# A recurrence fused with a two-layer MoE block: the first token sets worked in halves of four heads, and a plan with other transfer times

## The chip, the cores and the metric

The kernel runs on one core of one Trainium2 chip. The metric is the time on the device of one execution, in microseconds (us). A profiled execution is taken by the hardware profiler; its span runs from the first to the last instruction, and the execution's own time is a little longer.

The engines are named as in the profile: PE (matrix products; PEld its weight loads), DVE and ACT (elementwise work), POOL (elementwise work, here casts), SP (it issues the DMA transfers). Each takes its instructions in the order in which the program lists them, and an instruction that waits holds up those behind it.

## The reference

Inputs are q, k, v, alpha of shape 4 x 8 x 768 x 48 (batch, head, step, width) in float32, w_in (384 x 2048) and w_out (2048 x 384). Cut to what matters:

```python
def _attn_ref(q, k, v, alpha):
    state = np.zeros((B, H, D, D))
    for t in range(S):
        state = alpha[:, :, t, :, None] * state + np.einsum('bhd,bhe->bhde', k[:, :, t], v[:, :, t])
        y[:, :, t] = np.einsum('bhd,bhde->bhe', q[:, :, t], state)
    return y

def _moe_ref(x, w_in, w_out):
    r = np.maximum(x @ w_in, 0.0)
    return (r * r) @ w_out

x = attn_out.transpose(0, 2, 1, 3).reshape(B * S, H * D)     # 3072 tokens x 384
return _moe_ref(x, w_in, w_out)
```

## The kernel before

**Chunks.** The 3072 tokens are 24 chunks of 128, six to a batch. Within a chunk the recurrence is worked as products: L = ln(alpha), running sums of L over the tokens (a triangular matrix as stationary operand), A = exp(sum) and Ainv = exp(-sum), qA = q*A, kI = k*Ainv (scaling), scores = kI qA^T under a triangular mask (sm), and the outputs are sm times v plus qA times the state of the chunk before. The state is a product of kI and v, added in PSUM, scaled by exp of the chunk's total sum (ae) on DVE (L483, L660) and copied to bf16 on ACT (sb, L488, L665). The outputs are cast (xn), turned by PE and copied into xT_big (xT), the moving operand of the first MoE layer.

**Token sets.** The first four chunks come as two sets of 256 tokens (add_set, L336 on, loads in add_load2, L324 on). A set is loaded with two neighbouring tokens in one partition, so that a contiguous piece in memory is 384 bytes and not 192; j (0 or 1) names the even or the odd token. One load brings 384 KB: all eight heads, both j. add_set works by j: sums, exps and scalings for j = 0 and j = 1, transposes of q (L249) and of k for both j into one bank, copies (cast2, L409, L411) by j, scores by j, with all four head pairs of one j in a tile of two PSUM banks, and masked by mask_eo[j] (L452). The later chunks (add_chunk) are worked one by one.

**MoE.** The first layer (add_moe1) takes a group of chunks (GN: 4, 1, 1, 2, ...), and for each of 16 column blocks f of w_in makes three products of 128 x 256 (or 128) into a bank, relu on ACT (r, L744) and a square on DVE (gT, L753). Group 0 is worked as two pairs of chunks (lo = 0 and 2), and the products of pair 1 stand behind those of pair 0 in one chain. The second layer (add_moe2) makes for each chunk 16 products of 128 x 384 from gT and w_out; in group 0 it goes by quarters of four, each for all four chunks, so that the first quarter needs only the first quarter of w_out. The four chunks hold banks 4, 3, 2, 1 from their first quarter to their last.

**Weights.** w_in comes in five parts (column blocks 0 to 1, 2 to 3, 4 to 7, 8 to 11, 12 to 15), w_out in four; each is a load into one of four staging buffers and a cast to bf16 on POOL (load_w, L293, L296). The cast of a part gives its staging buffer back to the fourth load behind it.

**What sets the order.** A planner (class Plan) is run while the program is built. Every piece of work is an Op with an engine (or a choice of two), an assumed duration, dependencies, a priority and, where it needs one, a PSUM bank (takes; gives names the work that frees it). The planner takes the op that can start first, priority breaking ties, and the result, sorted by start, is the order of the program on all engines. The loads go through one planned DMA server in the order of DMA_ORDER, with assumed times LD (0.98, later LD1 = 1.0) for a load of one chunk, LD2 = 1.4 for a load of a set, WLD = 2.1 for a part of weights; SP issues them in that order. The times are assumed only in the plan: on the chip an instruction waits for what it really needs. A gate lets the recurrence run some 3.5 chunks ahead of the MoE work (LEAD).

**Opening.** PE first makes nine products on zeros into bank 4 (four columns of 128), and in planned gaps ahead of the first second-layer product more of 256 columns; their tile is named warm.

**PSUM.** Of eight banks, ps_sc holds the scores (two banks), ps_st the state (one), and banks[0] to banks[4] the rest: 0 and 1 for the recurrence (GLA_BANKS), 2 to 4 for the MoE.

The lines of the profile that the text speaks of: L331 (loads of a set), L318 (of a chunk), L293 and L296 (weights), L346 and L561 (Ln), L374 (exps of a set), L378 (its scalings), L351 (its cast of v), L246 and L249 (the helpers mm and tr, all products and all transposes).

Of the kernel before, what the change touches and what calls it, by code (L numbers as in the profile page):

```python
# [36 lines left out]
PE_CALM = 25.0  # L37


class Op:  # L40


    def __init__(self, eng, dur, emit, deps=(), prio=0.0, takes=None, gives=None, lat=None, at=0.0):
# [9 lines left out]
        self.start = self.done = None  # L53


def after(op, x=0.0):
    return (op, x)


class Plan:  # L60


    def __init__(self):
        self.pending = {}
        self.order = []
        self.free = {}

# [6 lines left out]
    def ready(self, op):  # L74
# [11 lines left out]
        if op.takes is not None:  # L86
            best = None
            for sl in op.takes:
                f = sl.free_at()
                if f is not None and (best is None or f < best):  # L90
                    best, op.slot = f, sl
            if best is None:
                return None
            t = max(t, best)
        return t

    def run(self, gate):
        free = self.free
        while any(self.pending.values()):
# [25 lines left out]
            op.start = t + getattr(op, "late", 0.0)  # L125
            free[eng] = t + op.dur
# [5 lines left out]
            if op.takes is not None:  # L132
                self.ready(op)
                op.slot.release.append(op.gives if op.gives is not None else op)
# [6 lines left out]
def kernel(  # L141
# [40 lines left out]
    ps_sc = ctx.enter_context(tc.tile_pool(name="ps_sc", bufs=1, space=PSUM))  # L182
    ps_st = ctx.enter_context(tc.tile_pool(name="ps_st", bufs=1, space=PSUM))
    banks = [ctx.enter_context(tc.tile_pool(name=f"bank{i}", bufs=1, space=PSUM)) for i in range(5)]
# [37 lines left out]
    mask_eo = [consts.tile([P, 1, 2, HP], BF16, name=f"mask{j}") for j in range(2)]  # L222
    for a in range(2):
        nc.vector.tensor_copy(mask_eo[0][:, 0, a, :], tri)
        nc.vector.tensor_copy(mask_eo[1][:, 0, a, :], tri if a else stri)
# [26 lines left out]
    sl_sc = Slots(1)  # L252
# [3 lines left out]
    GLA_BANKS = sl_bank[0:2]  # L256
    M1_BANKS = sl_bank[2:5]
    M2_BANKS = sl_bank[4:1:-1]

    def psum(op, shape, dt):  # L260
        i = op.slot.bank
        return banks[i].tile(shape, dt, name=f"bank{i}")
    X_SLACK = 0.2
    LD = 0.98
    LD1 = 1.0
    LD2 = 1.4
    WLD = 2.1
# [10 lines left out]
    def load_w(which):  # L278
# [19 lines left out]
        ld = add("DMA", WLD * n / 4 + 0.03, e_issue, prev, lat=2.0)  # L298
        op = add("POOL", 0.1 + 0.5 * n, e_cast, ld, prio=-3.0)
# [11 lines left out]
    def add_load(s, nm):  # L311
# [8 lines left out]
        d["ld_" + nm] = add("DMA", LD if s < 4 else LD1, ld, prev, lat=2.4 if s < 6 else 4.0, at=0.6)  # L320
# [3 lines left out]
    def add_load2(u, nm):  # L324
        d = E[u]

        def ld():
# [3 lines left out]
            pin(nc.sync.dma_start(out=t.rearrange("p (h e) -> p h e", h=H), in_=srcs2[nm][b, c // 2]))  # L331
        d["ld_" + nm] = add("DMA", LD2, ld, lat=2.5, at=0.6)

    def add_set(u):
# [7 lines left out]
        g = dict(prio=-10.0 + s0 * 0.01)  # L342
        R = [slice(HP * c, HP * c + HP) for c in range(2)]

        def e_ln():
            pin(nc.scalar.activation(L[:, :, :, 0:D], d["at"].rearrange("p h j d -> p j h d"), AF.Ln))  # L346
        ln = add("ACT", 0.85, e_ln, d["ld_at"], prio=-15.0)
# [4 lines left out]
        vb = add("POOL", 1.1, e_vb, d["ld_vt"], prio=-5.0)  # L352

        pm, A, Ai, exA, exI, mq, mk = {}, {}, {}, {}, {}, {}, {}

        def add_sum(j):
            def e_p0():
                pm[j] = psum(p0, [P, 512], FP32)
                cross = strict if j == 0 else incl
                mm(pm[j][:, 0:HD], lhsT=incl, rhs=L[:, 0, :, 0:D], start=True, stop=False)  # L360
                mm(pm[j][:, 0:HD], lhsT=(strict if j == 0 else incl), rhs=L[:, 1, :, 0:D], start=False, stop=True)
                if j == 0:
                    for p in range(NP):
                        for i in range(2):
                            mm(pm[j][:, HD + 2 * p:HD + 2 * p + 2], lhsT=L[:, i, 2 * p:2 * p + 2, :], rhs=half,
# [527 lines left out]
```

## Time and profile before

| | |
|---|---|
| runs | 193.73, 192.82, 193.62 us; median 193.62 |
| profiled execution | 192.82 us, span 191.1 us, mean granted clock of PE 0.997 |
| busy, share of the span | PE 95%, PEld 71%, DVE 68%, ACT 64%, POOL 14% |
| DMA | 30.22 MB, 158 GB/s in the mean; busy tenths 9 in the second to the twenty-fifth of 40 slices, but for two in between (7 and 8) |
| chain that ended last | PE 70%, DMA 15%, SP's queue 7%, DVE 2%, ACT 2% |
| ACT waits for alpha, chunks from the fifth on | 8.6 us in six waits, the longest 3.1 |

The page cuts the span into 40 slices of 4.78 us, with a digit for the busy tenths of each. PE's row is 7 to 9 in all but the last slice; in the first four slices a part of that is the products on zeros. The chain is followed back from the last instruction, at each step to what released it. In an answer by stretches each line has the stretch, its length and each engine's busy time, with the number of instructions in brackets. In a timeline a line has the start, the duration, the engine, the line of the kernel, the operation, out<-in and the shape; in square brackets stand the idle time before it and what ended it.

### The profile page before, as it was taken

How to read it: one execution, taken by the hardware profiler on the slowest of the kernel's cores; microseconds unless marked ns; L12 is line 12 of the kernel's file. 1: busy time of each engine (PE TensorE's matmuls, PEld its weight loads, DVE VectorE, ACT ScalarE, POOL GpSimd, SP SyncE). 2: the span in 40 equal slices, each digit the busy share in tenths (PEclk: the TensorE clock that was granted, in tenths of full speed). 3: DMA queues.
4: the chain of work that ended last, by engine and by line, in shares of the span. 5: the costliest groups of instructions: out<-in, count | busy, mean ns of one | idle time of the engine just before them, and what ended most of it. 6: DMA issues, size and time to landing. Idle time of an engine off the chain costs nothing.

```text
span 191.1 us, 5139 instructions
## 1 busy us (share of the span) xinstructions
PE 181.2 (95%) x2048; PEld 134.9 (71%) x2048; DVE 129.2 (68%) x280; ACT 121.6 (64%) x282; POOL 27.2 (14%) x44
## 2 busy tenths in 40 slices
PE   7887999989999799999999999999999999999992
PEld 2556788756887678767868768768778778668651
DVE  5478879634898888677878858758858858724200
ACT  3675589435986696854886956857857747628321
POOL 4015661641101111120110011011010000000000
PEclk9999999999999999999999999999999999999998
DMA  6999999999789999999999999860020020021012
GB/s 151 261 263 363 384 197 300 309 183 189 165 186 191 178 227 183 186 194 202 212 206 183 226 166 220 167 159 5 0 82 3 2 86 2 5 81 41 29 57 82
DMA packets 99176, 30.22 MB, mean 158 GB/s; under 512 B 92112, under 2 KB 98000, under 8 KB 99152
## 3 DMA queue, kind: packets, MB, share of 16 engines
q1 hardware_dynamic: 99152, 29.89, 71.6%
q8 instruction: 16, 0.26, 0.6%
q14 instruction: 8, 0.07, 0.1%
HBM read 25.17 MB, written 4.72 MB: 156 GB/s over the span
## 4 chain that ended last, share of the span: by engine, by line
PE 70%; DMA 15%; SPq 7%; DVE 2%; ACT 2%; POOL 1%; issue 1%; ACTq 0%
PE bank L246 61%; DMA at_s<-in_alpha_dram 7%; PE bank L249 6%; SPq L331 5%; DMA wo<-in_moe_w_out_dram 4%; DMA wi<-in_moe_w_in_dram 4%; PE sc L246 3%; SPq L293 1%; PE st L246 1%; POOL w_out_b L296 1%; DVE sm L640 1%; ACT r L744 1%; SPq L793 1%; POOL w_in_b L296 0%; DVE qkT L556 0%
## 5 line engine op out<-in xcount | busy, mean ns | idle before, releaser
L246 PE MATMUL bank<-xT_big,w_in_b 128*128 128x256 bf16 (+1 forms) x624 | 75.9, 264 | 0.5
L246 PE MATMUL bank<-w_out_b,gT 128*128 128x384 bf16 x384 | 71.6, 326 | 0.0
L744 ACT ACTIVATE r<-bank 128x512 bf16<-128x512 f32 x96 | 56.6, 600 | 17.7 <-PE bank L246 15.1
L246 PEld LDWEIGHTS <-w_in_b 128*128 128x128 bf16 x624 | 53.5, 97 | 8.9 <-issue 1.0
L753 DVE TENSOR_TENSOR gT<-r 128x512 bf16<-128x512 bf16 x96 | 41.4, 447 | 12.8 <-ACT r L744 12.0
L246 PEld LDWEIGHTS <-gT 128*128 128x128 bf16 x384 | 34.9, 98 | 18.5
L640 DVE TENSOR_TENSOR sm<-sc,utri_b 128x512 bf16<-128x512 f32 x40 | 25.7, 684 | 5.6 <-PE sc L246 5.6
L566 POOL CAST vb<-vt_s 128x384 bf16<-128x384 f32 x20 | 10.6, 530 | 93.4 <-DMA vt_s<-in_v_dram 48.3
L785 ACT COPY ob<-bank 128x384 f32<-128x384 f32 x23 | 11.1, 481 | 18.7 <-PE bank L246 18.6
L556 DVE COPY qkT<-bank 128x1024 bf16<-128x1024 bf16 x20 | 13.8, 689 | 5.0 <-PE bank L249 5.0
L554 ACT CAST xn<-bank 128x384 bf16<-128x384 f32 x20 | 9.5, 477 | 11.1 <-PE bank L246 11.1
L561 ACT ACTIVATE L_s<-at_s 128x384 bf16<-128x384 f32 x20 | 10.4, 522 | 8.9 <-DMA at_s<-in_alpha_dram 8.6
L556 DVE COPY xT_big<-bank 128x384 bf16<-128x384 bf16 x20 | 7.1, 354 | 13.1 <-PE bank L249 13.1
L599 DVE TENSOR_TENSOR qA_s<-qt_s,A 128x384 bf16<-128x384 f32 x20 | 11.6, 580 | 4.5 <-ACT A L580 3.8
L246 PEld LDWEIGHTS <-qkT 64*128 64x128 bf16 (+1 forms) x228 | 9.2, 95 | 6.1 <-issue 3.9
L602 DVE TENSOR_TENSOR kI_s<-kt_s,Ainv 128x384 bf16<-128x384 f32 x20 | 11.1, 556 | 0.3 <-ACT Ainv L584 0.3
L580 ACT ACTIVATE A<-bank 128x384 bf16<-128x384 f32 x20 | 9.8, 492 | 0.7 <-PE bank L246 0.7
L584 ACT ACTIVATE Ainv<-bank 128x384 bf16<-128x384 f32 x20 | 10.0, 498 | 0.0
L246 PE MATMUL bank<-vb,sm 128*128 128x48 bf16 (+1 forms) x224 | 9.7, 183 | 0.0
L249 PE MATMUL bank<-ident_bf,qA_s 128*128 128x128 bf16 x96 | 9.0, 219 | 0.7 <-DVE qA_s L378 0.7
L660 DVE TENSOR_TENSOR st<-st,ae_s 128x384 f32<-128x384 f32 x16 | 8.9, 558 | 0.6 <-PE st L246 0.6
L246 PEld LDWEIGHTS <-sm 128*128 128x128 bf16 (+1 forms) x224 | 8.4, 95 | 1.2 <-issue 0.4
(75 smaller groups left out, 162.2 us busy)
## 6 DMA issues: line engine op xcount, KB each, us to landing
at_s<-in_alpha_dram SPq DMA_DIRECT2D x20, 192.0 KB, 4.5
qt_s<-in_q_dram SPq DMA_DIRECT2D x20, 192.0 KB, 4.5
kt_s<-in_k_dram SPq DMA_DIRECT2D x20, 192.0 KB, 4.4
vt_s<-in_v_dram SPq DMA_DIRECT2D x20, 192.0 KB, 4.2
out_dram<-ob SPq DMA_DIRECT2D x20, 192.0 KB, 1.9
wo<-in_moe_w_out_dram SPq DMA_DIRECT2D x4, 768.0 KB, 7.8
wi<-in_moe_w_in_dram SPq DMA_DIRECT2D x3, 768.0 KB, 8.0
at_s<-in_alpha_dram SPq DMA_DIRECT2D x2, 384.0 KB, 5.0
```

What stands on the lines that cost most here:

```text
L246: pin(nc.tensor.matmul(*a, **kw))
L249: pin(nc.tensor.transpose(*a))
L556: pin(nc.vector.tensor_copy(out_t, in_t))
L561: pin(nc.scalar.activation(L[:, :, 0:D], d["at"], AF.Ln))
L566: pin(nc.gpsimd.tensor_copy(d["vb"], d["vt"]))
L584: pin(nc.scalar.activation(d["Ai"], d["pm"][:, 0:HD].rearrange("p (h d) -> p h d", h=H), AF.Exp, scale=-1.0))
L599: pin(nc.vector.tensor_mul(qA[:, :, 0:D], d["qt"], d["A"]))
L602: pin(nc.vector.tensor_mul(kI[:, :, 0:D], d["kt"], d["Ai"]))
L640: pin(nc.vector.tensor_mul(d["sm"][:, hh], d["sc"][:, hh], utri_b.to_broadcast([P, NP, P])))
L744: pin(nc.scalar.activation(box["r"][:, 0:w], box["ph"][:, 0:w], AF.Relu))
L753: pin(nc.vector.tensor_mul(dst, r, r))
L785: pin(nc.scalar.copy(box["ob"], box["po"]))
```

## The change

- A set is worked by halves a of four heads (two head pairs), both j together: Ln, sums, exps, scalings, turns, copies, scores and masks are done for half 0 and half 1. The chunk totals (e_tot) become a PE op of their own that needs both Lns and the Ainv exp of half 0. The outputs of a chunk are made in two ops (p3b, p3c), one behind each half's masks.
- Set 0's loads of alpha, q and k come in halves (a = 0 for the three, then a = 1); v of set 0 and all of set 1 come whole. SP issues 11 loads for the sets in place of 8. The bytes and the pieces of 384 bytes are the same.
- ps_sc goes; its two banks become banks[5] and banks[6]. A score op takes two banks (n_slots = 2), each freed by its own mask product. Sets draw every bank from SET_BANKS (0 to 3, 5, 6 for set 0; 0 to 2, 5, 6 for set 1), later chunks take 5 and 6 for scores. The last two groups may use all seven banks (M2_LAST).
- k's scaling in a set runs on DVE only; before, POOL was a choice.
- Group 0: each pair of chunks has a first-layer chain of its own (b1 = None per pair).
- The plan: LD1 1.1, LD2 1.5, WLD 2.05 for w_in and 2.4 for w_out with 0.85 of it for a short part, casts on POOL at 0.32 per block in place of 0.5, some other durations; DVE ops flagged shared (scalings and squares) are planned longer by 0.7 of the time that POOL works beside them; the state ops of sets get a priority ahead of the set's others; PE's planned start is 4.69, behind the opening products.
- Eight opening products in place of nine.

```diff
         if op.takes is not None:
-            best = None
-            for sl in op.takes:
-                f = sl.free_at()
-                if f is not None and (best is None or f < best):
-                    best, op.slot = f, sl
-            if best is None:
+            free = [(sl.free_at(), i) for i, sl in enumerate(op.takes)]
+            free = sorted((f, i) for f, i in free if f is not None)[:op.n_slots]
+            if len(free) < op.n_slots:
                 return None
-            t = max(t, best)
+            op.slots = [op.takes[i] for _, i in free]
+            op.slot = op.slots[0]
+            t = max(t, free[-1][0])
...
+            if eng == "POOL":
+                self.pool.append((t, t + op.dur))
+            elif eng == "DVE" and op.shared:
+                for a, z in self.pool[-3:]:
+                    op.dur += POOL_SHARE * max(0.0, min(z, t + op.dur) - max(a, t))
...
-    for a in range(2):
-        nc.vector.tensor_copy(mask_eo[0][:, 0, a, :], tri)
-        nc.vector.tensor_copy(mask_eo[1][:, 0, a, :], tri if a else stri)
+    mask_eo = consts.tile([P, 1, 2 * P], BF16)
+    for i in range(4):
+        nc.vector.tensor_copy(mask_eo[:, 0, HP * i:HP * i + HP], stri if i == 2 else tri)
...
         sl.bank = i
     GLA_BANKS = sl_bank[0:2]
+    SC_BANKS = sl_bank[5:7]
+    SET_BANKS = [sl_bank[0:4] + sl_bank[5:7], sl_bank[0:3] + sl_bank[5:7]]
...
-    LD1 = 1.0
-    LD2 = 1.4
-    WLD = 2.1
+    LD1 = 1.1
+    LD2 = 1.5
+    WLD = {"i": 2.05, "o": 2.4}
...
-        ld = add("DMA", WLD * n / 4 + 0.03, e_issue, prev, lat=2.0)
-        op = add("POOL", 0.1 + 0.5 * n, e_cast, ld, prio=-3.0)
+        ld = add("DMA", WLD[which] * (0.85 if n < 4 else n / 4.0), e_issue, prev, lat=2.2)
+        op = add("POOL", 0.1 + 0.32 * n, e_cast, ld, prio=-3.0)
...
+        lo, hi = (0, H) if a is None else (H // 2 * a, H // 2 * a + H // 2)
...
+            pin(nc.sync.dma_start(out=t.rearrange("p (h e) -> p h e", h=H)[:, lo:hi], in_=srcs2[nm][b, c // 2][:, lo:hi]))
+        op = add("DMA", LD2 * (hi - lo) / H, ld, lat=2.5, at=0.6)
+        for x in ([0, 1] if a is None else [a]):
+            d["ld_" + nm, x] = op
...
+        def add_decay(a):
+            def e_ln():
+                pin(nc.scalar.activation(L[:, :, heads[a], 0:D], d["at"][:, heads[a]].rearrange("p h j d -> p j h d"), AF.Ln))
+            ln[a] = add("ACT", 0.42, e_ln, d["ld_at", a], prio=-15.0)
+
...
+                pm[a] = psum(p0[a], [P, 512], FP32)
+                for j in range(2):
+                    for i in range(2):
+                        mm(pm[a][:, j * HW:j * HW + HW], lhsT=strict if i > j else incl, rhs=L[:, i, heads[a], 0:D],
+                           start=(i == 0), stop=(i == 1))
+            p0[a] = Op("PE", 0.33, e_p0, [ln[a]], takes=SET, lat=0.05, **g)
...
+            exA[a] = add("ACT", 0.38, lambda: e_exp(A, "A", 1.0), p0[a], **g)
+            exI[a] = add("ACT", 0.38, lambda: e_exp(Ai, "Ainv", -1.0), p0[a], **g)
+            p0[a].gives = exI[a]
+
+            def e_mul(dst, src, t):
+                pin(nc.vector.tensor_mul(dst[:, :, heads[a], 0:D], d[src][:, heads[a]].rearrange("p h j d -> p j h d"), t[a]))
+            mq[a] = add("DVE", 0.47, lambda: e_mul(qA, "qt", A), exA[a], d["ld_qt", a], **g)
+            mk[a] = add("DVE", 0.47, lambda: e_mul(kI, "kt", Ai), exI[a], d["ld_kt", a], **g)
+            mq[a].shared = mk[a].shared = True
...
+        def e_tot():
+            for p in range(NP):
+                for i in range(2):
+                    mm(pm[0][:, HD + 2 * p:HD + 2 * p + 2], lhsT=L[:, i, 2 * p:2 * p + 2, :], rhs=half,
+                       start=(i == 0), stop=(i == 1))
+        tot = plan.add(Op("PE", 0.34, e_tot, [ln[0], ln[1], exI[0]], lat=0.05, **g))
...
+        def add_turn(a, src, ready, out, q):
+            box = {}
+
+            def e_p1():
+                box["t"] = psum(p1, [P, NPH, 2, P], BF16)
+                for x, p in enumerate(pairs[a]):
+                    for j in range(2):
+                        tr(box["t"][:, x, j, :], src[:, j, 2 * p:2 * p + 2, :], ident_bf)
+            p1 = plan.add(Op("PE", 0.22, e_p1, [ready], takes=SET, lat=0.15, **g))
+
+            def e_cp():
+                if "qT" not in d:
+                    d["qT"] = work.tile([P, NP, 2, 2, HP], BF16, name="qT2", bufs=2)
+                    d["kT"] = work.tile([P, NP, 2, P], BF16, name="kT2", bufs=2)
+                x = slice(NPH * a, NPH * a + NPH)
+                if q:
+                    cast2(out[a], d["qT"][:, x], box["t"].rearrange("q p j (c i) -> q p c j i", c=2))
+                else:
+                    cast2(out[a], d["kT"][:, x], box["t"])
+            out[a] = add({"ACT": 0.49, "DVE": 0.34}, 0, e_cp, p1, **g)
+            p1.gives = out[a]
...
+                sc[a] = [psum(p2, [P, NPH, 2, P], FP32, hh) for hh in range(2)]
+                for x, p in enumerate(pairs[a]):
+                    for j in range(2):
+                        for c in range(2):
+                            for hh in range(2):
+                                r = slice(64 * hh, 64 * hh + 64)
+                                mm(sc[a][hh][R[c], x, j, :], lhsT=kT[r, p, j, R[c]], rhs=qT[r, p, c, :],
+                                   start=True, stop=True, tile_position=(64 * hh, 64 * c))
+            p2 = Op("PE", 0.45, e_p2, [cq[a], ck[a]], takes=SET, lat=0.10, **g)
+            p2.n_slots = 2
...
+                    sm[a] = work.tile([P, 2, NPH, 2, P], BF16, name="sm")
+                pin(nc.vector.tensor_mul(sm[a][:, hh].rearrange("p n j t -> p n (j t)"),
+                                         sc[a][hh].rearrange("p n j t -> p n (j t)"), mask_eo.to_broadcast([P, NPH, 2 * P])))
...
+            p2.gives = [s0_, s1_]
...
+            p3b = plan.add(Op("PE", 0.27, lambda: e_p3b(0), [smo[0], vb, after(p3a) if p3a else None],
+                              takes=SET if first else None, lat=0.05, **g))
+            p3c = plan.add(Op("PE", 0.27, lambda: e_p3b(1), [smo[1], after(p3b)], lat=0.15, **g))
...
-    DMA_ORDER = [("s", 0), ("s", 1), "i", "i", "i", "i", "i", "o", 4, "o", "o", "o", 5]
+    A0, B0, Z0 = [("at", 0, 0), ("qt", 0, 0), ("kt", 0, 0)], [("at", 0, 1), ("qt", 0, 1), ("kt", 0, 1)], [("vt", 0, None)]
+    A1, Z1 = [("at", 1, None), ("qt", 1, None), ("kt", 1, None)], [("vt", 1, None)]
+    DMA_ORDER = A0 + B0 + Z0 + A1 + Z1 + ["i", "i", "i", "i", "i", "o", 4, "o", "o", "o", 5]
...
             for lo in range(0, GN[0], 2):
+                b1 = None
                 for f in range(0, FT, 2):
                     b1 = add_moe1(g, f, b1, lo, lo + 2, per=2)
...
+    OPENING = 8
+    plan.free["PE"] = 1.25 + 0.43 * OPENING
     plan.run(gate)
```

## The prediction

> **What bounds the kernel now.** I read the busy row first (PE 95% of the span, DVE 68%, ACT 64%), then the chain of waits (PE 70%, DMA 15%, SP's queue 7%), then the timeline of the first 40 us, then busy time by stretches, cut where the timeline changes character. In the stretches the first number is the length, the second PE's busy time.
>
> ```profile
> core 0: us, PE busy (x) PEld busy (x) DVE busy (x) ACT busy (x) POOL busy (x), PEclk, DMA share, GB/s
> 9.60:18.86 9.26, 7.29 (x136) 5.42 (x136) 7.54 (x15) 6.04 (x15) 3.27 (x5) 1.00 1.17 311
> 18.86:22.20 3.34, 3.25 (x61) 2.37 (x61) 2.80 (x6) 1.87 (x4) 2.06 (x2) 1.00 1.04 387
> 22.20:31.00 8.80, 8.70 (x108) 7.31 (x109) 7.20 (x16) 7.15 (x17) 4.51 (x3) 1.00 0.94 237
> 31.00:35.20 4.20, 4.20 (x48) 3.38 (x48) 4.14 (x9) 3.58 (x7) 1.98 (x2) 1.00 1.05 380
> 35.20:40.00 4.80, 4.07 (x39) 2.53 (x37) 1.29 (x4) 1.05 (x3) 2.94 (x2) 1.00 1.02 223
> 40.00:60.00 20.00, 19.96 (x276) 15.50 (x274) 15.10 (x31) 14.04 (x36) 2.15 (x4) 1.00 1.04 187
> 60.00:82.00 22.00, 20.69 (x243) 16.25 (x241) 17.22 (x37) 16.48 (x41) 2.86 (x5) 1.00 1.05 192
> 82.00:187.70 105.70, 105.65 (x1107) 78.41 (x1105) 68.78 (x143) 66.32 (x155) 5.09 (x10) 1.00 0.50 106
> ```
>
> From the first MoE product at 18.86 to the last at 187.7, PE idles 0.09 + 0.10 + 0 + 0.73 + 0.04 + 1.31 + 0.05 = 2.32 us. Behind 18.86 nothing else is to be had: time can only come from useful products that run earlier than 18.86 (or take the place of other work soon after it), and from those 2.32 us. So the opening decides, and this is what it waits for (start, duration, then what):
>
> ```profile
> 4.62 0.84 ACT L346 ACTIVATE L_s<-at_s 128x768 bf16<-128x768 f32 x1 [2.54 <-DMA at_s<-in_alpha_dram]
> ...
> 10.64 0.84 ACT L346 ACTIVATE L_s<-at_s 128x768 bf16<-128x768 f32 x1
> ...
> 16.27 0.83 POOL L296 CAST w_in_b<-wi 128x768 bf16<-128x768 f32 x1 [0.29 <-DMA wi<-in_moe_w_in_dram]
> ...
> 18.62 0.83 POOL L296 CAST w_in_b<-wi 128x768 bf16<-128x768 f32 x1 [1.52 <-DMA wi<-in_moe_w_in_dram]
> ...
> 18.86 0.82 PE L246 MATMUL bank<-xT_big,w_in_b 128*128 128x256 bf16 x6
> ...
> 25.71 0.36 DVE L411 COPY xT_big<-bank 128x384 bf16<-128x384 bf16 x1
> ...
> 33.72 1.47 POOL L296 CAST w_out_b<-wo 128x1536 bf16<-128x1536 f32 x1 [1.98 <-DMA wo<-in_moe_w_out_dram]
> ...
> 39.15 0.52 ACT L561 ACTIVATE L_s<-at_s 128x384 bf16<-128x384 f32 x1 [3.06 <-DMA at_s<-in_alpha_dram]
> ...
> 39.72 0.32 PE L246 MATMUL bank<-L_s,utri_b 128*128 128x384 bf16 x1 [0.73 <-ACT L_s L561]
> ...
> 65.47 0.52 ACT L561 ACTIVATE L_s<-at_s 128x384 bf16<-128x384 f32 x1 [1.59 <-DMA at_s<-in_alpha_dram]
> ...
> 66.41 0.34 PE L249 MATMUL bank<-ident_bf,xn 128*128 128x128 bf16 x3 [1.15 <-ACT xn L554]
> ```
>
> To see: the first weights are cast by 17.1, 1.76 us before the first MoE product, so at 18.86 tokens are late, not weights. Set 1's tokens are there only at 26.07. The second part of w_out is cast at 35.2 and not sooner. And in the in-order queues of ACT and PE, work that the plan placed too early waits for a load: 0.73 us of PE at 39, 1.15 at 66.
>
> **The change part by part.**
>
> *Half loads.* The loads of at, q, k of set 0 are issued in halves (SP: 8 issues become 11). The loads of alpha for sets 0 and 1 land 3.8 and 6.2 us after their issues at 0.80 and 4.45, at 4.6 and 10.65: four loads of 384 KB in 6.05, 1.51 each. A half is 0.75, so the first lands at about 3.85, q and k halves at 4.6 and 5.4, second halves at 6.1, 6.9, 7.6; v of set 0 and all of set 1 land when they did, as the bytes ahead of them are the same. Three more issues cost 3 x 0.44 (the shortest issue here, the first) = 1.3 us of SP. They are hidden: SP's issues take 1.44 us each from 4.45 on, the pace of the landings, so SP waits for the queue. Were that cover gone, all weights would come 1.3 us later and the opening would give 1.3 less; the least is nothing. I take 0.
>
> *Set 0 in halves.* Ln of a half costs 0.52 (the 128x384 row of L561), two are 1.04 against 0.84: 0.2 more ACT per set, beside other work. The four exps, four scalings, four copies, four mask products of a set stay, 128x384 or 128x512 elements each. The chain of the first half, from rows: Ln to 4.4, the decay sums after the eight opening products (8 x 0.427 from 1.25: 4.67), exp 5.9 and 6.3, scaling (0.56) to 6.95, turn, copy 0.41 to 7.75, scores 8.0, masks (0.64 to 0.69) to 9.4. It ends beside the second half's loads. The second half's masks end near 12.4, the state step's 0.55 (DVE) and 0.48 (ACT) in between; then xn 0.48, turn 0.33, xT 0.48: 14.1 and 14.6 for the two chunks, against 17.75 and 18.81. This is 2.5 us ahead of the weights, so the first product starts at about 17.1; the halves of set 0 earn no more than 1.76 us, whatever they save.
>
> *Set 1.* Its loads end at 13.6 (k) and 15.1 (v). The four scalings end near 14.7, copies 15.3, four masks 2.7 us of DVE, two state steps 1.1, the squares of the first products (0.45 each) between them: masks done near 19, xT at 20 to 21 against 26.07. DVE from 5.4 to 20.5 holds two sets of about 6.7 (2.2 scalings, 2.7 masks, 1.1 state, 0.8 copies) and four squares of 0.45: 15.2 of 15.1 us. It is full; that is why I take 21 and not 20. The scaling that POOL did (0.91 at 13.97) comes to DVE at 0.56, and two DVE scalings beside POOL's work took 0.86 and 1.17 in place of 0.56; about even.
>
> *First layer in a chain per pair.* Before, pair 1's products stood behind all of pair 0's, hence behind the last w_in cast at 26.19. Now they go as soon as set 1 is there. By 22.2 PE before had done 12 MoE products; it still owed set 1 the mask products and turns (32 x 25 ns + 6 x 56 ns = 1.1 us). After, by 22.2, set 1 is done and 24 products are through (all that the four column blocks cast by 19.46 allow): 12 x 109 ns = 1.3 us more. Lead 2.4 us.
>
> *What is late next.* From 22.2 after owes 72 products of the first layer (7.85 us), the first quarter of w_out (16 x 162 ns = 2.6), chunk 4's own work (8 turns, 8 scores, state, sums, outputs: 1.65), 12.1 us, and some 0.1 us at each of eight changes between them: 22.2 + 12.9 = 35.1. The second quarter needs the cast at 35.2. It cannot be used sooner, so the lead at 35.2 is what before still owed then: 12 second-layer products of the first quarter (1.94) and chunk 4's last outputs (0.37), 2.3. Bounds: 2.3 above; below 0.7, if set 1 ends at 23.5. I take 1.9, nearer the top, as loads and weights come at known times and only DVE can slip.
>
> *Plan's transfer times.* Chunk 5's alpha was planned too early: the new costs move it by 8 x 0.1 (sets) + 1.1 (w_in: 9.63 against 8.55) + 1.1 (w_out) + 4 x 0.1 (chunk 4) + 0.2 = 3.6 us, and ACT's wait for it was 3.06. So the sums of chunk 5 go behind second-layer work that is ready; I take 0.7 of 0.73 (bounds 0 and 0.73). For chunk 10's alpha the shift is 5.4 with twenty more loads at 0.1, against a wait of 1.59. The 1.31 us of 60 to 82 can go, but a new order brings waits of its own: between 1.31 less and 1.31 more, I take 0.7 less.
>
> *Scores in two banks, shared flags, other plan costs.* Two banks before and after; each is freed by its own mask product. In steady state nothing waits for the scores' bank (PE idles 0.05 in 105.7), so 0.
>
> *One opening product fewer.* PE reaches the decay sums at 4.67 and not 5.09. The row: the granted clock is full from 5.5 on. [...]
>
> Sum: 192.82 (the profiled execution, 191.1 of span and 1.7 around it) - 1.9 - 0.7 - 0.7 = 189.5. That execution is the fastest of three; the median 193.62 stands 0.8 higher. Against the median: 190.3; I say 190.2.
>
> **The rivals.** 0.5%, 1 us here, is about what a measurement of this kernel tells from no change.
> - *DVE holds set 1 back* to 23 or later. For it: 15.2 us of work in 15.1. Against: half of the copies may go to ACT (6.04 busy of 9.26). Opening 0.7, plan 0.7: 193.62 - 1.4 = 192.2; between this and the forecast lies 191.
> [...]
> - *The lead is given back to the loads*: DMA is busy all through to 130 us and its stream does not move, and alpha was waited for six times by ACT, 8.6 us in all, between 39 and 82. If PE, 1.9 ahead, meets loads that are no earlier, it loses the lead, not more: 193.6. Against: PE needs 7.0 us per chunk, loads come every 4.5, so the early chunks alone are exposed, and the plan now knows their times.
> - *Slower: loads behind outputs.* The plan now charges 4 x 1.1 + 0.55 = 4.95 us per chunk where the trace shows 4.5, so from chunk 10 on the plan's loads drift by 0.45 a chunk, and in SP's queue each goes behind more output issues that wait for evictions. Before, loads were issued some 8 us ahead of their Ln (chunk 22: 114.07 against 122.77). Twelve chunks of drift are 5.4, leaving 2.6; it decides if the drift passes 0.7 a chunk. Four late chunks at 1.3 us each (the stall at 66): 190.2 + 5.2 = 195.4.
> - *Sync at the seams.* More interleaving means more 0.1 us changes; ten would take 1 us: 191.2, inside the forecast's range.
>
> **How the numbers follow.** Forecast (188.6 to 191.6) 0.58; DVE holds set 1 (191 to 192.6) 0.20; clock 0.04; lead given back 0.08; slower 0.10. Faster by over 0.5% is below 192.65: 0.58 + 0.20 + 0.04 + a little of the fourth = 0.83; slower, over 194.6, 0.10; between, 0.07. The range: the low end takes every bound at its best, 193.62 - 2.3 - 0.73 - 1.31 = 189.3, and 1.8 for the small waits and for runs that differ by 0.9; the high end takes DVE's case with room: 187.6 to 193.0.
>
> **What would show it.** Right: first first-layer product near 17.1; set 1's last xT at 20 to 21.5; products of both pairs mixed before 26; first w_out product near 32; second quarter at 35.2, directly behind its cast; no PE idle over 0.3 us at 39 and 66. Wrong: a first product after 18, set 1 after 23, w_in or w_out casts over 0.5 us later than before, Ln waits longer than 8.6 us in all, or PE idle behind 18 above 2.3 us.

## The result and the profile after

| | before | after |
|---|---|---|
| median of four runs each, us | 193.31 (192.82 to 193.73) | 191.06 (190.79 to 191.5) |
| ratio of the times | | 0.9887, 95% interval 0.9852 to 0.9921 |
| profiled execution, us | 192.82, span 191.1 | 190.92, span 189.2 |
| PE idle from the first MoE product to the last, us | 2.32 | 1.09 |

The kernel is 1.1% faster: 2.25 us by the medians, 1.9 us between the two profiled executions. In the runs below, an execution that took over 1.5% longer than the fastest of its kernel is in the medians and ranges and not in the ratios. Forecast were 190.2 us and a gain of 3.4. The mechanism holds (useful products run earlier, and PE idles less). But two of the steps that carry it are wrong, and the runs below show that the part of the change with which the prediction began, the halves, is not needed for the gain.

The same stretches in the kernel after; only the first bound (the first MoE product) and the last differ. First number the length, second PE's busy time:

```profile
core 0: us, PE busy (x) PEld busy (x) DVE busy (x) ACT busy (x) POOL busy (x), PEclk, DMA share, GB/s
9.60:18.58 8.98, 7.87 (x159) 6.05 (x159) 8.18 (x17) 6.35 (x16) 2.48 (x3) 1.00 1.13 303
18.58:22.20 3.62, 3.62 (x66) 2.92 (x67) 2.96 (x6) 2.11 (x5) 2.25 (x2) 1.00 0.95 336
22.20:31.00 8.80, 8.74 (x84) 7.64 (x83) 7.26 (x13) 7.08 (x14) 4.71 (x5) 1.00 0.97 251
31.00:35.20 4.20, 4.20 (x42) 2.93 (x42) 3.98 (x8) 2.58 (x8) 1.32 (x2) 1.00 1.04 381
35.20:40.00 4.80, 4.80 (x48) 3.12 (x47) 1.65 (x3) 1.44 (x3) 3.39 (x3) 1.00 1.03 237
40.00:60.00 20.00, 19.59 (x257) 14.83 (x255) 14.32 (x30) 12.77 (x33) 1.70 (x4) 1.00 0.90 181
60.00:82.00 22.00, 21.43 (x267) 17.28 (x266) 20.17 (x44) 17.48 (x44) 3.26 (x5) 1.00 1.12 193
82.00:185.80 103.80, 103.75 (x1089) 77.43 (x1086) 65.03 (x140) 65.64 (x154) 5.99 (x11) 1.00 0.53 109
```

PE's idle time is 0 + 0.06 + 0 + 0 + 0.41 + 0.57 + 0.05 = 1.09 us. The 0.73 of 35 to 40 is gone, the 1.31 of 60 to 82 has become 0.57, and 40 to 60 has 0.41 where there was 0.04.

The timeline of the kernel after (start, duration, what; in brackets the idle time before and what ended it):

```profile
3.56 0.52 ACT L373 ACTIVATE L_s<-at_s 128x384 bf16<-128x384 f32 x1 [1.48 <-DMA at_s<-in_alpha_dram]
...
16.61 0.83 POOL L366 CAST vb<-vt_s 128x768 bf16<-128x768 f32 x1 [5.97 <-DMA vt_s<-in_v_dram]
...
17.70 0.83 POOL L305 CAST w_in_b<-wi 128x768 bf16<-128x768 f32 x1 [0.26 <-DMA wi<-in_moe_w_in_dram]
...
18.58 0.50 PE L254 MATMUL bank<-xT_big,w_in_b 128*128 128x256 bf16 x3 [0.59 <-POOL w_in_b L305]
18.75 0.83 POOL L305 CAST w_in_b<-wi 128x768 bf16<-128x768 f32 x1 [0.22 <-DMA wi<-in_moe_w_in_dram]
...
22.22 0.62 DVE L420 COPY xT_big<-bank 128x384 bf16<-128x384 bf16 x2 [0.21 <-PE bank L257]
...
32.65 0.82 PE L254 MATMUL bank<-w_out_b,gT 128*128 128x384 bf16 x4
34.37 1.47 POOL L305 CAST w_out_b<-wo 128x1536 bf16<-128x1536 f32 x1 [2.88 <-DMA wo<-in_moe_w_out_dram]
...
39.42 0.52 ACT L575 ACTIVATE L_s<-at_s 128x384 bf16<-128x384 f32 x1 [1.63 <-DMA at_s<-in_alpha_dram]
...
49.58 0.33 PE L257 MATMUL bank<-ident_bf,xn 128*128 128x128 bf16 x3 [0.41 <-DVE ob L801]
...
62.67 0.34 PE L254 MATMUL bank<-L_s,utri_b 128*128 128x384 bf16 x1 [0.45 <-DVE qkT L570]
```

To see: set 0 starts 1.1 us sooner (3.56 against 4.62), yet the first MoE product comes at 18.58, only 0.28 sooner than before, and this time it waits for weights: their first cast is at 17.70, not 16.27. Set 1's tokens are complete at 22.84 (before 26.07), and the first w_out product is at 32.65 (before 34.56). In the list of waits, ACT's waits for the alpha of later chunks fall from 8.6 us in six waits to

```profile
ACT L_s L575 <- DMA at_s<-in_alpha_dram: 2.0, 2, 1.6
```

**The lead of PE.** To see where the time goes, I count the useful products (without those on zeros) that each kernel has started by a moment, each at the time that its shape takes PE in the densest stretches (0.109 us for 256 columns, 0.162 for 384, and so on), and subtract. In us of PE work, the kernel after is ahead of the one before by 0.51 at 18.6, 1.0 from 31 to 38.6, 1.78 at 39.7 (before stood still at 39), 1.3 at 60, 2.0 at 66.5 and 1.94 at 180. So 1.0 of the 1.9 us comes from the opening, 0.8 from the stall at 39, and the rest is a gain at 65 and a loss between 40 and 62 that nearly cancel. In the sections below "lead" is this difference to the kernel before.

### The profile page after: what moved, and what is told of

Its sections match the earlier page's. It is cut to its first block, busy times and chain, and to the rows that moved or that the text cites. A ratio compares the mean times of both kernels' runs of the same rounds, so it can differ in the third digit from the quotient of the medians.

```text
span 189.2 us, 5166 instructions
## 1 busy us (share of the span) xinstructions
PE 181.8 (96%) x2056; PEld 136.5 (72%) x2056; DVE 129.4 (68%) x283; ACT 120.4 (64%) x282; POOL 27.0 (14%) x43
## 4 chain that ended last, share of the span: by engine, by line
PE 83%; SPq 5%; DVE 4%; DMA 4%; issue 1%; POOL 0%; ACT 0%; ACTq 0%; DVEq 0%
PE bank L254 75%; PE bank L257 7%; SPq L341 5%; DMA wi<-in_moe_w_in_dram 4%; PE st L254 1%; DVE gT L770 1%; DVE sm L657 1%; DVE kI_s L616 1%; DVE qA_s L613 1%; DVE qkT L570 0%; POOL w_in_b L305 0%; DVE ob L801 0%; ACT ob L803 0%; DVE st L677 0%; DVE xT_big L570 0%
## 5 line engine op out<-in xcount | busy, mean ns | idle before, releaser
L254 PE MATMUL bank<-xT_big,w_in_b 128*128 128x256 bf16 (+1 forms) x624 | 75.0, 264 | 0.6 <-POOL w_in_b L305 0.6
L770 DVE TENSOR_TENSOR gT<-r 128x512 bf16<-128x512 bf16 x96 | 42.1, 458 | 12.8 <-ACT r L761 12.4
L657 DVE TENSOR_TENSOR sm<-bank,utri_b 128x512 bf16<-128x512 f32 x40 | 25.6, 682 | 2.6 <-PE bank L254 2.4
L803 ACT COPY ob<-bank 128x384 f32<-128x384 f32 x22 | 10.5, 479 | 21.8 <-PE bank L254 21.7
L580 POOL CAST vb<-vt_s 128x384 bf16<-128x384 f32 x20 | 11.3, 564 | 90.8 <-PE bank L254 46.3
L682 ACT CAST sb<-st 128x384 bf16<-128x384 f32 x16 | 7.6, 476 | 4.9 <-DVE st L677 4.8
```

The costliest lines, as they stand in the source:

```text
L254: pin(nc.tensor.matmul(*a, **kw))
L580: pin(nc.gpsimd.tensor_copy(d["vb"], d["vt"]))
L657: pin(nc.vector.tensor_mul(d["sm"][:, hh], d["sc"][hh], utri_b.to_broadcast([P, NP, P])))
L770: pin(nc.vector.tensor_mul(dst, r, r))
L803: pin(nc.scalar.copy(box["ob"], box["po"]))
```

## The experiments

All kernels compute the whole reference; the one without products on zeros leaves out nothing else. Each time stands beside that of the kernel before in the same rounds. The changed kernel itself was run in the same rounds as the last three variants alone; elsewhere it is compared by its ratio to the kernel before, 0.9887 in the section above and 0.9924 in those rounds. Line numbers in rows of kernels made from the one before are its own (or one higher, where a line was added).

**New times alone.** The kernel before with only the plan's new transfer times:

```diff
-    LD1 = 1.0
-    LD2 = 1.4
-    WLD = 2.1
+    LD1 = 1.1
+    LD2 = 1.5
+    WLD = {"i": 2.05, "o": 2.4}
-        ld = add("DMA", WLD * n / 4 + 0.03, e_issue, prev, lat=2.0)
+        ld = add("DMA", WLD[which] * (0.85 if n < 4 else n / 4.0), e_issue, prev, lat=2.2)
-        ... lat=2.4 if s < 6 else 4.0, at=0.6)
+        ... lat=2.6 if s < 6 else 4.0, at=0.6)
```

> The kernel before with the new transfer times of the plan alone (one chunk's load 1.1, a set's 1.5, weights 2.05 and 2.4, landing 2.2 and 2.6). Theory A (two separate gains: the opening gives about 1.0 us, the plan's times about 0.9): the stalls of PE at 39 and at 66 go, ACT's waits for alpha fall from 8.6 us to under 4, the first first-layer product stays at 18.9, and the time is 192.3 (192.0 to 192.7) against 193.3. Rival B (the plan's times are the whole gain, the halves earn nothing because the weights hold the start): 191.2. Rival C (the times do nothing alone): 193.3.

Measured: 195.11 us beside 192.46, ratio 1.0157 (1.0086 to 1.0229). None of the expectations had a loss of this kind. Timeline and stretches of this kernel:

```profile
17.95 0.48 PE L246 MATMUL bank<-L_s,incl 128*128 128x384 bf16 x2
...
18.27 0.82 PE L246 MATMUL bank<-xT_big,w_in_b 128*128 128x256 bf16 x6
18.47 0.49 ACT L374 ACTIVATE A<-bank 128x384 bf16<-128x384 f32 x1 [2.13 <-PE bank L246]
```

```profile
18.27:26.00 7.73, 6.26 (x98) 4.68 (x96) 6.62 (x11) 4.65 (x12) 5.13 (x4) 1.00 1.11 357
35.20:40.00 4.80, 3.18 (x40) 2.25 (x39) 4.80 (x9) 2.56 (x5) 3.13 (x2) 1.00 1.03 218
60.00:82.00 22.00, 21.82 (x275) 17.17 (x273) 19.37 (x43) 17.24 (x42) 3.02 (x5) 1.00 1.10 191
```

The stall of 60 to 82 does go (0.18 left of 1.31), so the new times do what they were to do there. But the new order puts the second decay sum of set 1 at 17.95, where the kernel before had

```profile
12.48 0.50 PE L246 MATMUL bank<-L_s,incl 128*128 128x384 bf16 x2
```

The recurrence has two banks, 0 and 1, and in this order the outputs of set 0 have them first; the run with free banks below tests this. Set 1 comes late, PE idles 1.47 us in 18 to 26 and 1.62 in 35 to 40, and the lead is -3.0 at 26 and -4.1 at 38.6.

**Chain per pair alone.** The kernel before with

```diff
             for lo in range(0, GN[0], 2):
+                b1 = None
```

> The kernel before with a first-layer chain per pair of chunks alone. Theory A: set 1's tokens are there at 26.07 and the last part of w_in is cast at 26.19, so pair 1's products cannot use the freedom: 193.3 within 0.4. Rival B (the chain is what lets PE run ahead): at least 0.8 less, 192.5 or below, with products of pair 1 before pair 0's last.

Measured: 192.69 us beside 192.46, ratio 1.0000 (0.9968 to 1.0031); the lead is 0 from 28 to 60. The mixing is worth nothing where set 1's tokens come at 26 anyway.

**The changed kernel with the old times.** The first diff, turned round, in the kernel after:

```diff
-    LD1 = 1.1
-    LD2 = 1.5
-    WLD = {"i": 2.05, "o": 2.4}
+    LD1 = 1.0
+    LD2 = 1.4
+    WLD = 2.1
```

> The changed kernel with the old transfer times in the plan. Theory A: a stall for chunk 5's alpha near 39 and others up to 80 come back, 0.7 to 1.4 us, so 191.06 becomes 191.8 to 192.4, the opening up to 31 is as in the changed kernel. Rival B (times are the whole gain): 193 or more. Rival C (times do nothing): 191.1.

Measured: 193.55 us beside 192.46, ratio 1.0042 (1.0001 to 1.0084). Beside the changed kernel (0.9887) the loss is more than the 1.23 us of idle time that the old times could bring back. The stretches of its profiled execution (193.32) show one thing that adds to it:

```profile
9.00:20.03 11.03, 9.32 (x187) 6.64 (x187) 9.45 (x19) 7.04 (x18) 3.32 (x4) 1.00 1.13 315
20.03:26.85 6.82, 6.82 (x65) 5.02 (x63) 5.55 (x9) 2.24 (x6) 4.41 (x3) 0.50 1.05 313
```

The granted clock falls to half for 6.82 us, in the middle of the first layer. The lead goes from +0.53 at 18.6 to -1.42 at 26, is -1.83 at 38.6 and, as the order behind 39 is now the better one, +0.35 at 66.5. So this execution does not price the old times by themselves. But the clock is not the whole loss: six of the ten executions had a mean granted clock of 0.971 to 0.991, and the four at 1.0 took 192.08 to 193.2 us, 193.0 in the median, no less than the kernel before. With the old times the gain is gone at full clock too; no trace shows where it goes there.

**The changed kernel with set 0 loaded whole.**

```diff
-    A0, B0, Z0 = [("at", 0, 0), ("qt", 0, 0), ("kt", 0, 0)], [("at", 0, 1), ("qt", 0, 1), ("kt", 0, 1)], [("vt", 0, None)]
+    A0, B0, Z0 = [("at", 0, None), ("qt", 0, None), ("kt", 0, None)], [], [("vt", 0, None)]
```

> The changed kernel with set 0's alpha, q and k loaded whole, work still by halves of four heads. Theory A (more and smaller loads put the landings back by 0.57 us): v of set 0 lands at 9.1 and not 9.7, alpha of set 1 at 10.6 and not 11.2, later ones 0.5 earlier; set 0 starts 1 us later but stays covered by the weights; time 190.5 to 191.1. Rival D (the halves' early start is needed): set 0's outputs come after the first weights' cast, time 191.3 to 192.

Measured: ten runs from 191.91 to 197.35 us, 195.89 in the median, beside 192.46; the ratio of 1.0025 (0.9982 to 1.0069) rests on the four shortest. Nine of the ten had a mean granted clock of 0.972 to 0.991, and the one at 1.0 took 191.91. The profiled execution (195.37):

```profile
17.04:23.86 6.82, 6.66 (x84) 4.81 (x83) 3.99 (x7) 1.45 (x3) 4.47 (x5) 0.50 1.04 375
```

Again 6.82 us at half clock. The loss goes with the clock, which gave way in nine runs of ten: 193.0 to 194.0 us at a mean of 0.988 to 0.991, 195.4 to 197.35 at 0.972 to 0.982. At full clock there is a single run, 191.91. By its ratios the changed kernel would have taken 190.3 to 191.0 in these rounds, an estimate, so whole loads may cost 0.9 to 1.6 us at full clock.

**The changed kernel with two banks for the sets.**

```diff
-    SET_BANKS = [sl_bank[0:4] + sl_bank[5:7], sl_bank[0:3] + sl_bank[5:7]]
+    SET_BANKS = [GLA_BANKS, GLA_BANKS]
-            p2 = Op("PE", 0.45, e_p2, [cq[a], ck[a]], takes=SET, lat=0.10, **g)
+            p2 = Op("PE", 0.45, e_p2, [cq[a], ck[a]], takes=SC_BANKS, lat=0.10, **g)
```

> The changed kernel, its sets confined to the banks that they had before: two (0 and 1) for everything but scores, two (5 and 6) for scores. Theory E (the wider choice of banks is what makes the opening work: with two banks a sum of set 1 waits until an output of set 0 has left): set 1's exps start 2 us or more later, the 24th first-layer product comes after 25.5, and the time is 193 to 195. Rival F (banks cost nothing, as the prediction had it): 191.1 within 0.5.

Measured: 192.04 us beside 192.3, ratio 0.9982 (0.9949 to 1.0015). The gain is gone, though the loss is less than the banks' theory had (193 to 195). PE's stalls in its timeline:

```profile
23.18 0.44 PE L254 MATMUL bank<-vb,sm 64*128 64x48 bf16 x14 [0.38 <-DVE sm L464]
...
38.44 0.27 PE L254 MATMUL bank<-vb,sm 128*128 128x48 bf16 x4 [0.96 <-DVE sm L657]
```

The outputs of set 1 wait for its masks (L464), the 24th first-layer product comes at 25.18 and not 24.10, and at 38.44 chunk 4's masks are late: the lead is +0.62 at 20, -0.40 at 24, -1.40 at 38.6.

**New times with free banks, in the kernel before.** The first diff, and the sets' ops of the recurrence draw their banks from 0 to 3 (set 0) and 0 to 2 (set 1) in place of 0 and 1:

```diff
+        SET = [sl_bank[0:4], sl_bank[0:3]][u]
-            p0 = Op("PE", 0.6 if j == 0 else 0.35, e_p0, [ln], takes=GLA_BANKS, lat=0.05, **g)
+            p0 = Op("PE", 0.6 if j == 0 else 0.35, e_p0, [ln], takes=SET, lat=0.05, **g)
         (and so for the turns, both parts of the outputs and xT of a set)
```

> The kernel before with the new transfer times, and its sets free to use banks 0 to 3 (set 0) and 0 to 2 (set 1); no halves, no half loads, one chain. Theory E: the 3 us that the new times alone lost before 26 come back, and the stalls at 39 and 66 stay gone: 191.6 to 192.4. Rival G (the loss with the new times alone has another cause): 194 to 195.

Measured: 192.51 us beside 192.3, ratio 1.0000 (0.9964 to 1.0036). Beside the times alone (1.0157) this one edit takes the whole loss back: the banks were the cause. In its timeline the second decay sum of set 1 is back at 12.96, and the second line shows what holds the ratio at 1.00:

```profile
12.96 0.49 PE L246 MATMUL bank<-L_s,incl 128*128 128x384 bf16 x2
...
26.95 0.93 PE L246 MATMUL bank<-warm 128*128 128x256 bf16 x7 [0.69 <-ACT r L745]
```

At 26.95 PE has nothing but products on zeros: set 1's tokens are there, but pair 1's products stand behind pair 0's, whose weights are not. Lead +0.69 at 22.2, -1.42 at 28.

**The changed kernel with one chain.**

```diff
             for lo in range(0, GN[0], 2):
-                b1 = None
```

> The changed kernel with both pairs' first-layer products in one chain as before. Theory A: set 1 is ready at 22.9, three us before the last of w_in, so the freedom is worth what pair 1 does before 26.2: some 0.8 us; 191.6 to 192.2, PE idle between 22 and 27. Rival J (pair 0's products fill the time as well, since weights come in every 2 us): within 0.3 of 191.1.

Measured: 192.34 us beside 192.3, ratio 0.9991 (0.9963 to 1.0019), just above the 191.6 to 192.2 expected. Its timeline has the same hole at the same place:

```profile
26.71 0.81 PE L254 MATMUL bank<-warm 128*128 128x256 bf16 x6 [0.68 <-ACT r L761]
```

Lead +1.03 at 22.2, -1.09 at 28, -0.16 at the end.

**The changed kernel without products on zeros behind the opening.**

```diff
-    DUMMY = 1
+    DUMMY = 0
```

> The changed kernel without the products on zeros that fill PE's planned gaps in the opening (the eight opening ones stay). Theory H (the clock of PE in the opening hangs on how densely PE is filled): the granted clock falls to half for one or two stretches of 3.4 us before 26, mean clock 0.97 to 0.99, and the time is 1.5 to 3.5 above the changed kernel, 192.5 to 194.5. Rival I (the opening waits for loads and weights, a slow clock hides there): within 0.5 of 191.1. On the side: fewer instructions of PE, so the 16 KB transfer on the instruction queue that came at 12.97 comes later than 13.5, and v of set 1 lands before 16.5.

Measured: 194.23 us beside 192.3, ratio 1.0064 (1.0023 to 1.0106). The stretches of its profiled execution:

```profile
5.60:9.00 3.40, 1.72 (x36) 1.30 (x36) 2.46 (x6) 2.30 (x7) 0.00 (x0) 1.00 1.25 271
9.00:19.24 10.24, 9.52 (x122) 7.72 (x126) 7.97 (x15) 6.60 (x17) 2.70 (x4) 0.50 1.17 312
```

PE is busy for half of 5.6 to 9.0, and the clock is at half from 9.0 to 19.24. That does not explain the loss: seven of the ten executions had a mean granted clock of 0.962 to 0.982 and took 192.61 to 194.97 us, but the three at 1.0 took 194.77, 195.97 and 196.31. No trace of these three was kept, so what the products on zeros are worth, and by what, stays open. In this run v of set 1 lands at 15.37, earlier than in the kernel after (16.56); the last section comes back to that.

**The changed kernel again, on another chip**, as the base of the next three.

> The changed kernel once more, beside the others. Both theories: 190.4 to 191.4, 1 to 2 us below the kernel before in the same rounds (192.3 on the last chip). If it comes out within 0.5 us of the kernel before, the gain hangs on the chip, and what the parts are worth is smaller than the ledger of the traces says.

Measured: 191.41 us beside 192.84, ratio 0.9924 (0.9894 to 0.9955). First product at 18.14, lead +0.90 at 35.2, +1.62 at 39.7, +1.46 at 180: the gain and its places come again, a little smaller.

**New times, free banks and the chain per pair in the kernel before**: no halves, no half loads. The diff of the run with free banks, and b1 = None.

> The kernel before with three things: the new transfer times, banks 0 to 3 and 0 to 2 for the sets, a chain per pair. No halves of heads, no half loads. Theory K (the three act only together, and the halves add little, as weights hold the first product): no hole of PE between 25.9 and 27, PE's lead over the kernel before at 31 is 0.5 to 1.0 us, the time within 0.6 of the changed kernel. Rival L (the halves bring set 1 forward by the microsecond that counts): at least 0.8 above the changed kernel.

Measured: 191.56 us beside 192.84, ratio 0.9921 (0.9889 to 0.9952): the changed kernel's own gain. Stretches of this kernel:

```profile
18.86:22.20 3.34, 3.34 (x67) 2.63 (x66) 2.83 (x6) 1.56 (x3) 2.05 (x2) 1.00 1.04 386
22.20:31.00 8.80, 8.74 (x100) 7.51 (x95) 6.86 (x13) 7.32 (x15) 5.41 (x4) 1.00 1.00 251
35.20:40.00 4.80, 4.52 (x40) 2.92 (x39) 2.87 (x5) 1.00 (x2) 2.93 (x2) 1.00 0.99 200
40.00:60.00 20.00, 20.00 (x260) 15.14 (x259) 12.83 (x27) 13.28 (x33) 1.98 (x4) 1.00 1.02 184
60.00:82.00 22.00, 21.02 (x266) 17.10 (x265) 19.70 (x45) 17.68 (x45) 2.92 (x6) 1.00 1.18 201
```

The first product starts at 18.87, as in the kernel before, set 1's tokens are complete at 24.34, and PE is full to 31 but for 0.06 us all the same. The lead is smaller in the opening (+0.54 at 31) and as large at the end (+1.62 at 180, against +1.46 of the changed kernel beside it). What the halves win in the opening, they do not bring to the end, as far as the two intervals, 0.3% each way, can tell.

**The changed kernel with the first weights ahead of set 1's v.**

```diff
-    DMA_ORDER = A0 + B0 + Z0 + A1 + Z1 + ["i", "i", "i", "i", "i", "o", 4, "o", "o", "o", 5]
+    DMA_ORDER = A0 + B0 + Z0 + A1 + ["i"] + Z1 + ["i", "i", "i", "i", "o", 4, "o", "o", "o", 5]
```

> The changed kernel with the first part of w_in loaded ahead of v of set 1. Theory M (the start of the first layer waits for weights): the first weights land near 15.3 to 16.3 and the first product comes at 16.5 to 17.5, time 0.3 to 0.8 below the changed kernel. Rival N (set 1 is what PE waits for at 22, and v of set 1 is in its way): v a microsecond later, set 1 a microsecond later, time 0 to 1 above the changed kernel.

Measured: 191.3 us beside 192.84, ratio 0.9933 (0.9900 to 0.9965). In its timeline

```profile
17.49 0.83 PE L254 MATMUL bank<-xT_big,w_in_b 128*128 128x256 bf16 x6
```

the first product is 0.65 earlier than in the changed kernel beside it, set 1's tokens are later (they are turned at 23.21), and the lead at 31 is +0.87 and at the end +0.97. Starting the first layer sooner brought nothing here, where set 1 came later for it.

**The changed kernel with the opening's products cut in four.** 32 products of 128 columns in place of 8 of 512, the same 3.59 us:

```diff
-        mm(wp, lhsT=warm[:, 0:P], rhs=warm, start=True, stop=True)
+        for n in range(4):
+            mm(wp[:, n * P:n * P + P], lhsT=warm[:, 0:P], rhs=warm[:, 0:P], start=True, stop=True)
```

> The changed kernel with its eight opening products of 512 columns as 32 of 128: the same time, 48 more instructions of PE. Theory O (a 16 KB transfer on the instruction queue, PE's next instructions, holds one DMA engine for 1.1 us, and the load that is under way lands that much later): that transfer comes at 10.5 to 12.5 and no longer at 13 to 15.4, and a load of set 1 that landed in step in the other runs (q or k, 12.1 and 13.6) lands 0.7 to 1.2 late. Rival P (the late landing belongs to the place in the load order): the instruction transfer moves, v of set 1 or the first weights are the first late load as before. Time within 0.7 of the changed kernel.

Measured: 190.82 us beside 192.84, ratio 0.9902 (0.9867 to 0.9937). The interval overlaps the changed kernel's on the same chip (0.9894 to 0.9955), so I don't claim that it is faster. What it was made for is in the last section.

## Why the prediction was right, and where not

**Right: the bound.** PE was the bound from the first MoE product on, time could only come from products that run sooner or from the 2.32 us of idle time, and it came from there: 0.51 us of lead at the first product and 1.23 us less idle time behind it make 1.74 of the 1.9. The lead of the opening was not given back to the loads: +1.0 at 35.2, and ACT waits 2.0 us for alpha and not 8.6.

**The opening: 1.0 us, not 1.9.** The direction is the one described, set 1 sooner (22.84 against 26.07) and no longer behind all of pair 0's products; the term of the sum was mis-sized, inside its bounds (0.7 to 2.3). The 24 products forecast by 22.2 were 12, and the 24th started at 24.10, later than before (23.39). The step that failed is "v of set 0 and all of set 1 land when they did, as the bytes ahead of them are the same". The bytes moved were the same (worked out from the transfers, 1524 and 1521 KB by 8 us, 3055 and 3028 by 14), but set 0's v landed at 9.69 in place of 9.12, set 1's v at 16.56 in place of 15.10, and the first weights at 17.65 in place of 16.22. So the first product was held by weights to 18.58 and not by them at 17.1, and set 1, whose v was cast from 16.61 on, was complete at 22.84 and not at 20 to 21. The early part of this begins at the second half of set 0's alpha: a load has 16 landings in the trace, and from there on one of them is 0.5 us behind the other fifteen (6.68 against 6.18; for set 0's v 9.69 against 9.19). Whether the half loads bring that about is not shown: in six of the seven other runs with half loads set 0's v lands at 9.04 to 9.29, in one at 9.89, and in the six runs with whole loads at 8.96 to 9.12. What delays set 1's v further is in the last section. The price of three more issues was rightly 0: in those six runs set 0's v is at most some 0.3 later than with whole loads.

**The stall at 39: 0.7 forecast, 0.8 measured.** The lead grows from 0.97 to 1.78 across it. In the kernel before with the chain alone, the old plan, it is there (0.71 at 39.66, behind ACT's Ln).

**The stalls of 40 to 82: 0.7 forecast, 0.37 measured.** Idle time there went from 0.04 + 1.31 to 0.41 + 0.57, so 0.74 was won behind 60 and 0.37 lost ahead of it. As the prediction allowed, the new order has waits of its own: at 49.58 a turn behind DVE's ob, at 62.67 a sum behind DVE's qkT. DVE's busy time in 60 to 82 rose from 17.22 to 20.17 of 22.

**Wrong: "Scores in two banks, shared flags, other plan costs ... so 0".** The text looked at the steady state and at the scores, and never priced that a set may draw six banks (five for set 1) where it had two. This is the part without which the rest loses: the new times alone cost 2.65 us, with free banks 0.2 (ratio 1.0000), and the changed kernel with two banks for the sets keeps nothing of its gain (0.9982).

**Wrong: the halves as the source of the opening's gain.** "Set 0 in halves" was to bring the first product to 17.1. Times, banks and chain without any halves reach 0.9921, the changed kernel 0.9924 beside it. And none of the three can be left out: taken out of the changed kernel, the chain leaves 0.9991, the banks 0.9982, the times 1.0042; added to the kernel before, the chain alone gives 1.0000, the times alone 1.0157, times and banks 1.0000. The gain is of the three together: the times give an order that fits the loads, the banks let set 1 follow that order, and the chain lets PE use set 1's tokens while pair 0 waits for weights. Free banks alone, or with the chain and the old times, were not tried in the kernel before.

**The rivals.** *DVE holds set 1 back* is half seen: set 1 was 1.8 to 2.8 us later than forecast, with DVE at 8.18 of 8.98 us busy up to 18.58, but its v was itself 1.46 late. *The clock* opened later than the 5.5 that the prediction took: in the kernel after, products of 256 columns still start 0.21 us apart up to 6.35, against 0.11 from 6.36 on in the kernel before, and the trace grants full clock from 6.55 (in all kept traces from 5.04 to 7.25). It did not fall in the changed kernel's profiled executions; in one of its eleven executions, of 195.78 us, the mean was 0.982. It fell in the traces of three variants, for 6.8 to 10.2 us, and with the old times the lead went from +0.53 at 18.6 to -1.42 at 26. No run shows what the chance of 0.04 for the clock was worked out from; the kept traces show it full from 7.25 at the latest, and in three variants at half from 9.0, 17.04 and 20.03. *Loads behind outputs* did not come: PE's idle time behind 82 is 0.05. No loss by *sync at the seams* is seen: the 0.1 us that it counts on is there at some changes in the kernel before (twelve products of 0.109 us start at 22.18, the outputs behind them at 23.60) and not at others (three start at 25.01, a turn at 25.34).

**The marks.** Of those given for "wrong", the first product after 18 and casts over 0.5 late (17.70 against 16.27, 34.37 against 33.72) came true while the time stayed in its range. They marked a step as wrong, not the result; the second quarter of w_out started at 36.26, 0.4 behind the end of its cast. Of those given for "right", the first product near 17.1 (18.58), set 1's last xT at 20 to 21.5 (22.84) and the second quarter at 35.2 did not come; the first w_out product near 32 (32.65) and no stall at 39 did. The low end of the range, 189.3 less 1.8, is 187.5 and not 187.6, which changes nothing.

## What to carry to other kernels

Where a planner sets the order of in-order engines, correct costs can make the order worse if a resource that the order leans on (here two PSUM banks) is short: price what every new order holds, and how long, before pricing what it saves. A part that is worth nothing alone may be what another part needs, so test parts by taking each out of the whole as well as by adding each to the old kernel. And a step that starts the bound engine sooner pays only if the next late thing, here the second set of tokens and the weights behind it, comes sooner too.

## What the runs showed of the hardware

**One part of a load landed 0.85 to 1.54 us late beside a transfer on the instruction queue.** The page of the kernel after lists

```profile
q8 instruction: 16, 0.26, 0.6%
```

16 packets of 16 KB in the span. Each takes 0.88 to 1.38 us, the first one 1.19, and they come about 250 PE instructions apart, so I take them for PE's instructions. A load has 16 landings in the trace, one for each of its parts, and is complete with the last, so a mean rate says nothing of it. In all kept traces one part of a load falls 0.85 to 1.54 us behind the other fifteen shortly after the first packet, and is still behind in the loads that follow:

| kernel | first packet at | load | fifteen parts by | last part |
|---|---|---|---|---|
| before | 15.38 | second part of w_in | 17.23 | 18.57 |
| after | 12.97 | v of set 1 | 15.41 | 16.56 |
| without products on zeros | 14.48 | first part of w_in (v in step, 15.37) | 16.33 | 17.87 |
| two banks | 13.70 | first part of w_in (v in step, 15.02) | 16.10 | 16.97 |
| opening cut in four | 12.10 | v of set 1 | 14.93 | 15.86 |

In the kernel before the next two parts of w_in have 19.29 and 20.60, 21.32 and 22.64. The last row is the run made to move the packet: I had expected q or k of set 1 to be the late load. So packet and delay go together, and which load is hit first is not settled by the packet's start. Whether the packet and the late part share one DMA engine is not shown: the record of a packet does not name its engine.

**The clock was at half for 6.82 and 10.24 us, behind stretches in which PE was thin.** The stretches at half clock are 6.82 us twice and 10.24, that is 2 and 3 times 3.41. They come in three variants: no products on zeros, set 0 loaded whole, old times. In each, the 3.41 us just ahead of the fall are thin: PE is busy for 1.72, 2.27 and 2.19 us of them, against 2.75 or more in each of the four such stretches of the kernel after from 6.55 to 20.2. So PE was half to two thirds busy ahead of each fall. But a stretch like that did not bring a fall every time: 2.13 us of 3.41 at 36.53 with two banks, and 2.26 at 63.5 before, passed at full clock. What makes the clock fall is therefore not shown. A lower mean is not special to the variants: 10 of 25 executions of the kernel before, in the rounds of the first four variants, had a mean granted clock of 0.991, which is what 3.41 us at half clock would give (1.7 of 191 us, an estimate from the 3.41 above). What a fall costs is not settled: with whole loads the time rises with it, without products on zeros the executions at full clock were among the longest.
